# Linear attention woven into a feed-forward layer on one core: the second visit of attention split in two, and the copies of the solved values shared by two engines

## The chip, the cores and the metric

The program runs on one NeuronCore of a Trainium2 chip. Five engines work side by side, each through its own list of instructions in order: TensorE (PE in the tables; its weight loads stand apart as PEld), VectorE (DVE), ScalarE (ACT), GpSimd (POOL) and SyncE (SP, which here issues nearly all transfers). They meet only at semaphores. The metric is the device time of one execution in microseconds (us). Lower is better.

## The reference

Two parts, one behind the other. Attention is a delta rule with a state of 48x48 per head, for 4 batches, 8 heads and 768 positions:

```
k_n = k / (np.linalg.norm(k, axis=-1, keepdims=True) + 1e-06)
for t in range(S):
    y[:, :, t] = np.einsum('bhd,bhde->bhe', q[:, :, t], state)
    v_old = np.einsum('bhde,bhd->bhe', state, kt)
    state = state + bt[:, :, :, None] * np.einsum('bhd,bhe->bhde', kt, vt - v_old)
```

Its output, laid out as 3072 tokens of 384 numbers, goes through a feed-forward layer with 2048 inner columns:

```
h = np.maximum(x @ w_in, 0.0)
return (h * h @ w_out).astype(np.float32)
```

All is float32.

## The kernel before

The 768 positions are cut into 12 **units** of 64 (`u` = 0 to 11). Within a unit the recurrence is solved as a triangular system of 64 rows for each of the 32 pairs of batch and head. VectorE inverts the two 32-row halves of the triangle step by step (`invert`, L542 and L543), a unit ahead. TensorE puts the halves together and applies the result. The layer of unit `u - 1` runs on TensorE at the same time as the attention of unit `u`: the layer is long and made of large matmuls (128x128 weights, 256 or 384 columns), the attention is made of many small ones (32x32 to 64x64).

**The layer** (`moe`) of one unit has 8 rounds. A round makes one tile `h` with 18 matmuls (L756; in the changed file L762). ScalarE then takes Relu, Square and a rounded copy of it (`r`, `r`, `h_h`, L763 to L766), and VectorE the remainder (`h_l`, L735). Two rounds later 12 matmuls (L743; L749) add it to the outputs `o0` and `o1`.

**The attention** of a unit visits TensorE at fixed places between those rounds:

- first half of the corner: `h <- tt, ap` (L600; after the change L611), copied to `m` by ScalarE (L602);
- keys on the state: `x <- state, kq` (L639; L645), subtracted from the values `vt` by VectorE (L647);
- second half of the corner: `h <- m, t1` (L613; L623), written into `tt` by four ScalarE instructions (L617);
- queries on the state: `g <- state, kq` (L639; L645);
- the values solved: `x <- vt, tt` (L663; L669), copied back into `vt` (L665; L671);
- scores on them: `g <- vt, ap` (L677; L683), then keys on them, `x <- vt, kpad` (L695; L701), for the state.

The preparation of the unit two ahead (`prepared`, called `ahead`) takes a step behind some of these: transposes of its keys and queries (L353), two tiles into `x` and two into `h`, copied to `kq` by ScalarE (L356), then products of them (L369) and masked copies by VectorE (`ap`, L379). Units 10 and 11 have no unit to prepare.

**What sets the order.** The scheduler is off; every engine gets its instructions in the order in which the code issues them. `weave` merges generators by a table of places between 0 and 1. The layer has 32 places in a unit, and `CHAIN`, in 32nds, says where the attention comes in:

```
def two_visits(d, ahead):
    ahead = ahead or iter(())
    corner_rows(d)
    yield
    for _ in whole(d):
        pass
    take(ahead, 1)
...
CHAIN = (15.5, 17.5, 25.5)
```

So at 15.5 VectorE transposes the corner (`t1`, L563), at 17.5 the whole of `whole` is issued (the **second visit**), and at 25.5 everything from the solved values on (the **third visit**). The tile `h` has two buffers in PSUM, shared by the layer, both halves of the corner and the transposes; `x` has two of its own. Each of these buffers is handed on in turn.

Of the kernel before, what the change touches and what calls it, by code (L numbers as in the profile page):

```python
# [8 lines left out]
F32 = mybir.dt.float32  # L9
# [12 lines left out]
def kernel(  # L22
# [22 lines left out]
    nc = tc.nc  # L45
    B, H, S, D = q.shape
    DM, DF = w_in.shape
    P = 128
    C = 64
    HB = 32  # L50
# [11 lines left out]
    apool = ctx.enter_context(tc.tile_pool(name="attn", bufs=2))  # L62
# [34 lines left out]
    ttile = []  # L97
    for i in range(2):
        tt = const.tile([P, NC, H, C], F32, name=f"tt{i}")
# [212 lines left out]
    def x_tile(u=2):  # L312

        turn[0] += 1
        pool, name = (ps_h, "h") if u <= 1 and split_early and turn[0] % 4 >= 2 else (ps_x, "x")
        return pool.tile([P, PC], F32, name=name)
# [243 lines left out]
    def corner_rows(d):  # L560

        d["t1"] = apool.tile([P, H, HB], F32, name="t1", bufs=1)
        nc.vector.transpose(out=d["t1"], in_=d["t1t"])  # L563
        return d["t1"]

    def whole(d):

        u, ap = d["u"], d["ap"]
        tt = ttile[u % 2]
        upper = [slice(b * C, b * C + HB) for b in range(2)]  # L570
        lower = [slice(b * C + HB, (b + 1) * C) for b in range(2)]

        if not u:

            low, t1 = d["low"], d["t1"]
            m = mpool.tile([P, H2, HB], F32, name="x_l", bufs=1)
            ps = ps_h.tile([P, PC], F32, name="h").rearrange("p (h t) -> p h t", h=H2)
            for h in range(H2):
                for b in range(2):
                    nc.tensor.matmul(ps[upper[b], h], lhsT=ap[lower[b], h // H, h % H, 0, :HB], rhs=low[lower[b], h],  # L580
                                     start=True, stop=True)
            for b in range(2):
                nc.scalar.copy(out=m[upper[b]], in_=ps[upper[b]])
            yield
            ps = x_tile(u).rearrange("p (h t) -> p h t", h=H2)
            for h in range(H2):
                for b in range(2):
                    nc.tensor.matmul(ps[upper[b], h], lhsT=t1[upper[b], h], rhs=m[upper[b], h], start=True, stop=True)
            for b in range(2):
                nc.scalar.mul(out=tt.rearrange("p c h t -> p (c h) t")[upper[b], :, HB:], in_=ps[upper[b]], mul=-1.0)  # L590
            yield
            return
        t1 = d["t1"] if "t1" in d else corner_rows(d)
        m = apool.tile([P, H, HB], F32, name="m", bufs=1)
        at = [upper, lower]
        ps = ps_h.tile([P, PC], F32, name="h")[:, :H * HB].rearrange("p (k t) -> p k t", k=H)
        for h in range(H2):
            c, e = h // H, h % H
            for b in range(2):
                nc.tensor.matmul(ps[at[h % 2][b], h // 2], lhsT=ap[lower[b], c, e, 0, :HB],  # L600
                                 rhs=tt[lower[b], c, e, HB:], start=True, stop=True)
        nc.scalar.copy(out=m, in_=ps)  # L602
        if u == 1:
            yield
        keys_on_state(d)
        if u < MERGED - 2:
            yield
        ps = [(x_tile(u) if u < MERGED - 2 else ps_h.tile([P, PC], F32, name="h"))[:, :H * HB]
              .rearrange("p (k t) -> p k t", k=H) for _ in range(2)]
        for h in range(H2):  # L610
            for b in range(2):  # L611
                rows = at[h % 2][b]
                nc.tensor.matmul(ps[h % 2][upper[b], h // 2], lhsT=t1[rows, h // 2], rhs=m[rows, h // 2], start=True, stop=True)  # L613
        right = tt.rearrange("p c (k j) t -> p j (c k) t", j=2)
        for j in range(2):
            for b in range(2):
                nc.scalar.mul(out=right[upper[b], j, :, HB:], in_=ps[j][upper[b]], mul=-1.0)  # L617
        if u == 1:
            yield
        queries_on_state(d)  # L620
        yield

    def areas(two, n):  # L623

        return [x[:, :NC * n * D].rearrange("p (c n e) -> p c n e", c=NC, n=n) for x in two]

    def by_parity(x):

        return [x.rearrange("p c (n j) e -> p j c n e", j=2)[:, j] for j in range(2)]
# [12 lines left out]
    def keys_on_state(d):  # L642

        ks = areas([x_tile() for _ in range(2)], NP)
        on_state(d, 0, ks)  # L645
        for left, old in zip(by_parity(d["vt"]), ks):
            nc.vector.tensor_tensor(out=left, in0=left, in1=old, op=ALU.subtract)  # L647

    def queries_on_state(d):

        d["g"] = g = ps_g.tile([P, 2, PC], F32, name="g")
        on_state(d, 1, areas([g[:, j] for j in range(2)], NP))

    def solved(d):

        u, vt, tt = d["u"], d["vt"], ttile[d["u"] % 2]
        tv = areas([x_tile(u) for _ in range(2)], NP)
        for c in range(NC):
            for h in range(H):
                p, j = h // 2, h % 2  # L660
                for b in range(2):
                    rows, to = slice(b * C, (b + 1) * C), slice((b ^ j) * C, ((b ^ j) + 1) * C)
                    nc.tensor.matmul(tv[j][to, c, p], lhsT=tt[rows, c, h], rhs=vt[rows, c, h], start=True, stop=True)  # L663
        for new, old in zip(by_parity(vt), tv):
            nc.scalar.copy(out=new, in_=old)  # L665

    def scores_on_solved(d):

# [117 lines left out]
    def take(gen, n=None):  # L786
        while n is None or n > 0:
            try:
                next(gen)
            except StopIteration:  # L790
                return
            if n is not None:
                n -= 1
# [40 lines left out]
    def state_part(d):  # L834
        yield from whole(d)
        solved(d)
        yield
        onward(d)
        yield

    def two_visits(d, ahead):

        ahead = ahead or iter(())
        corner_rows(d)
        yield
        for _ in whole(d):
            pass
        take(ahead, 1)
        yield
        solved(d)  # L850
        take(ahead, 1)
        scores_on_solved(d)
        take(ahead, 1)
        if d["u"] < units - 1:
            keys_on_solved(d)
        yield
# [1 line left out]
    STEPS = 32  # L858
    OVER = 4
    MERGED = 4  # L860
    CHAIN = (15.5, 17.5, 25.5)
    CHAIN1 = (14.4, 17, 19.5, 21.5, 23.5, 27)
    L1, N1, N2 = 0.01, (0.36, 0.76), (0.03, 0.42)
    NI, SPANS = HB, {1: (0.54, 1.14), 2: (0.5, 1.12)}
# [1 line left out]
    ds_ = []  # L866
# [4 lines left out]
    with tc.manual_schedule(engines=engines):  # L871
# [47 lines left out]
        chain = state_part(ds_[0])  # L919
# [27 lines left out]
        for u in range(1, units):  # L947
            parts = []
            begun, ended = SPANS.get(u, (0.42, 1.1))
            n_i = round((1 - begun) / (ended - begun) * NI)  # L950
            if inverse:
                parts.append((inverse, left))
            getting, now = loads(u), moe(ds_[u - 1]) if u > 1 else first
            parts += [(now, [-2])] if u > 1 else []
            if u < MERGED - 1:
                parts.append((static(ds_[u + 1]), [-1, 0.155, 0.165, 0.17] if u > 1 else [0.12, 0.2, 0.21, 0.215]))
            elif ahead:
                parts.append((ahead, [-1, 0.13, 0.17]))
            ahead = prepared(u + 2) if 1 < u < units - 2 else None
            inverse = invert(ds_[u + 1]) if u < units - 1 else None  # L960
            if inverse:
                parts.append((inverse, steps(n_i, begun, 1)))
                left = steps(NI - n_i, 0, ended - 1) + [0.16 if u == 1 else 0.15]
            if u == 1:
                parts.append((corner, [0.04, 0.09, 0.1]))
                parts.append((third, [0.01, 0.015, 0.03, 0.045]))
                parts.append((late_loads(), [0.08]))
                parts.append((splits, steps(3 * (NW - FIRST) + 3 - used, 0, 0.72)))
                parts.append((pair[1], [0.25]))
            parts.append((getting, [L1] + steps(6, *N2) + [0.72, 0.93] if u + 2 < units else []) if u > 1 else  # L970
                         (getting, [0.09] + steps(6, *N1) + [0.93, 0.94]))
            chain = two_visits(ds_[u], ahead) if u > 1 else state_part(ds_[u])
            parts.append((chain, [x / STEPS for x in (CHAIN if u > 1 else CHAIN1)]))
            if before:
                parts += [(before, [x / STEPS for x in range(OVER)] + [0.2, 0.21])]
            parts.append((now, [x / STEPS for x in range(OVER, STEPS)] if u > 1 else steps(STEPS - OVER, 0, 1)))
            weave(*parts)
            before = now
# [34 lines left out]
```

## Time and profile before

| | before |
|---|---|
| median of three timed runs | 659.32 us (657.95 to 663.64) |
| the profiled execution | 661.13 us, of it span 659.4 us |
| TensorE busy | 601.3 us, 91% of the span |
| VectorE busy | 426.2 us, 65% |
| ScalarE busy | 317.2 us, 48% |
| mean granted TensorE clock | 0.951 of full speed |

The span is the time between the first and the last instruction of the profiled execution. An engine's busy time is the sum of its instructions. The granted clock is what the throttle let TensorE have: 1.00 is 2.4 GHz and 0.50 is 1.2 GHz. One profiled execution is one sample; the median of three others stands beside it.

### The profile page before, as it was taken

What the parts mean: (1) busy time and instruction counts of PE and PEld (TensorE: products, weight loads), DVE (VectorE), ACT (ScalarE), POOL (GpSimd) and SP (SyncE); (2) the same over time, 40 slices, a digit from 0 to 9 for tenths busy, and PEclk for the clock granted to TensorE, in tenths of its full rate; (3) what the DMA queues carried; (4) which work ended last, traced back from release to release, by engine and by line L of the source; (5) the groups of instructions that cost most, each with busy time, mean ns of one, the idle gap of its engine ahead of it and who ended that gap; (6) DMA issues with size and microseconds to landing.
All of it is one profiled execution on the core that took longest, in us unless ns stands there. A gap on an engine that the chain in (4) does not pass through costs nothing.

```text
span 659.4 us, 23855 instructions
## 1 busy us (share of the span) xinstructions
PE 601.3 (91%) x10392; PEld 570.6 (87%) x10392; DVE 426.2 (65%) x1131; ACT 317.2 (48%) x621; POOL 30.8 (5%) x52
## 2 busy tenths in 40 slices
PE   2948898998998999999999999999999999998997
PEld 2537787998998998998998998998998998898996
DVE  4795878886487676576587676775875855831121
ACT  4746675555345354354354354445444343354442
POOL 4000100001001000010001010010010010000000
PEclk9957697998999997998999999999999997999999
DMA  7797544035235244143134253143161051030100
GB/s 233 180 273 159 179 85 86 16 63 109 41 52 103 45 79 78 29 88 73 29 75 82 45 88 70 36 84 73 35 107 33 3 110 29 2 65 3 25 1 24
DMA packets 172464, 49.31 MB, mean 75 GB/s; under 512 B 164288, under 2 KB 167368, under 8 KB 172360
## 3 DMA queue, kind: packets, MB, share of 16 engines
q1 hardware_dynamic: 168840, 47.06, 34.1%
q8 instruction: 81, 1.33, 0.8%
q10 hardware_dynamic: 3392, 0.72, 0.6%
q14 instruction: 23, 0.19, 0.1%
q0 software_dynamic: 128, 0.01, 0.0%
HBM read 36.54 MB, written 10.49 MB: 71 GB/s over the span
## 4 chain that ended last, share of the span: by engine, by line
PE 80%; ACT 10%; issue 4%; DMA 3%; DVE 2%; SPq 1%; ACTq 0%; DVEq 0%
PE o L743 32%; PE h L756 31%; PE g L639 2%; PE x L369 2%; ACT r L764 2%; PE g L677 2%; ACT r L763 2%; ACT h_h L766 2%; PE x L353 1%; PE h L613 1%; PE x L695 1%; DMA kpad<-in_k_dram 1%; ACT vt L665 1%; PE h L722 1%; PE h L353 1%
## 5 line engine op out<-in xcount | busy, mean ns | idle before, releaser
L743 PE MATMUL o<-w,h_h 128*128 128x384 f32 x768 | 205.9, 350 | 0.0
L756 PE MATMUL h<-x_h,w 128*128 128x256 f32 x1152 | 170.7, 284 | 0.0
L763 ACT ACTIVATE r<-h 128x512 f32<-128x512 f32 x96 | 57.4, 598 | 231.6 <-PE h L756 231.2
L735 DVE TENSOR_TENSOR h_l<-r,h_h 128x512 fp32r<-128x512 f32 x96 | 68.3, 711 | 150.9 <-ACT h_h L766 150.3
L756 PEld LDWEIGHTS h<-x_h,w 128*128 128x128 f32 x1152 | 157.1, 192 | 0.6
L743 PEld LDWEIGHTS o<-w,h_h 128*128 128x128 f32 x768 | 139.0, 193 | 2.4
L743 PE MATMUL o<-w,h_l 128*128 128x384 f32 x384 | 132.4, 345 | 0.0
L542 DVE SCALAR_TENSOR_TENSOR tmp<-lt,bt,z 128x126 f32<-128x126 f32 (+22 forms) x310 | 96.8, 312 | 10.9 <-DMA lt<-blocks 2.6
L756 PE MATMUL h<-x_l,w 128*128 128x256 f32 x576 | 100.3, 283 | 0.0
L543 DVE TENSOR_TENSOR z<-z,tmp 128x126 f32<-128x126 f32 (+22 forms) x310 | 79.2, 255 | 10.7
L756 PEld LDWEIGHTS h<-x_l,w 128*128 128x128 f32 x576 | 82.8, 191 | 0.0
L743 PEld LDWEIGHTS o<-w,h_l 128*128 128x128 f32 x384 | 74.1, 193 | 0.0
L764 ACT ACTIVATE r<-r 128x512 f32<-128x512 f32 x96 | 60.7, 632 | 3.1
L766 ACT CAST h_h<-r 128x512 fp32r<-128x512 f32 x96 | 59.6, 620 | 3.0
L531 POOL MEMSET z<- 128x512 f32 x10 | 5.3, 527 | 470.9 <-DMA inv<-z 272.4
L677 PE MATMUL g<-vt,ap 64*64 64x48 f32 x768 | 17.7, 221 | 7.7 <-ACT vt L665 5.4
L677 PEld LDWEIGHTS g<-vt,ap 64*64 64x64 f32 x768 | 14.6, 134 | 10.7 <-ACT vt L665 8.6
L700 DVE TENSOR_TENSOR state<-state,x 48x384 f32<-48x384 f32 x40 | 22.0, 550 | 2.6 <-PE x L695 2.0
L356 ACT COPY kq<-x 128x512 f32<-128x512 f32 x25 | 13.6, 592 | 16.1 <-PE x L353 16.1
L369 PE MATMUL x<-kq 48*64 48x64 f32 (+1 forms) x608 | 19.5, 256 | 1.2 <-ACT kq L356 0.7
L617 ACT ACTIVATE tt<-h 32x256 f32<-32x256 f32 x40 | 14.9, 373 | 11.6 <-PE h L613 11.2
L639 PE MATMUL g<-state,kq 48*64 48x48 f32 x704 | 16.0, 237 | 4.5 <-issue 4.5
(147 smaller groups left out, 644.9 us busy)
## 6 DMA issues: line engine op xcount, KB each, us to landing
w<-in_moe_w_in_dram SPq DMA_DIRECT2D x12, 512.0 KB
w<-in_moe_w_out_dram SPq DMA_DIRECT2D x16, 384.0 KB
lt<-blocks SPq DMA_DIRECT2D x20, 256.0 KB
qpad<-in_q_dram SPq DMA_DIRECT2D x96, 48.0 KB
vt<-in_v_dram SPq DMA_DIRECT2D x48, 96.0 KB
out_dram<-a SPq DMA_DIRECT2D x46, 96.0 KB
kpad<-in_k_dram SPq DMA_DIRECT2D x88, 48.0 KB
blocks<-ap SPq DMA_DIRECT2D x40, 64.0 KB
```

The lines of the kernel that those rows point to most:

```text
L369: nc.tensor.matmul(ps[j][to * C:(to + 1) * C, p, (x - first) * C:(x - first + m) * C], lhsT=kq[rows, c, p, b, 0], rhs=kq[rows, c, p, b, x: ...
L542: nc.vector.scalar_tensor_tensor(out=tmp, scalar=bt[:, s:s + 1], op0=ALU.mult, op1=ALU.mult, **factors)
L543: nc.vector.tensor_tensor(out=z[:, :nj, s + 1:], in0=z[:, :nj, s + 1:], in1=tmp, op=ALU.subtract)
L639: nc.tensor.matmul(dst[j][to, c, p], lhsT=d["kq"][rows, c, p, b, x], rhs=state[rows, b, c, p], start=(c == 0 and p == 0) if x else True, s ...
L677: nc.tensor.matmul(gy[j][to, c, p], lhsT=ap[rows, c, h, 1], rhs=uu[rows, c, h], start=(u == 0 and c == 0 and p == 0), stop=True, skip_grou ...
L700: nc.vector.tensor_tensor(out=state[rows, b], in0=state[rows, b], in1=ku[b][rows], op=ALU.add)
L735: nc.vector.tensor_tensor(out=h_l, in0=r, in1=h_h.bitcast(F32), op=ALU.subtract)
L743: nc.tensor.matmul(o[i], lhsT=a[:, e, i * P:(i + 1) * P], rhs=halves["wo", ft][w], start=(ft == 0 and n == 0), stop=(ft == FT - 1 and n == 2))
L756: nc.tensor.matmul(hp[:, e], lhsT=halves["wi", (kt, ft // EACH)][w][:, f], rhs=x[:, kt], start=(n == 0), stop=(n == 3 * KT - 1))
L763: nc.scalar.activation(out=r, in_=hp, func=AF.Relu)
L764: nc.scalar.activation(out=r, in_=r, func=AF.Square)
L766: nc.scalar.copy(out=h_h, in_=r)
```

## The change

The second visit is cut. Its first half (first half of the corner, keys on the state) is issued at 15.5, one `h` group of the layer earlier than before. The transposed corner `t1` is made at 16.5. The second half of the corner, the queries and the step of `ahead` follow at 19.5, behind one `h` group and 12 `o` matmuls of the layer. The third visit stays at 25.5; for units 10 and 11, which prepare nothing, the scores and what follows are issued at 27.5. Of the two copies of the solved values, the one for odd heads goes to VectorE (units 2 to 11). Unit 0 and unit 1 keep their order.

```
-        t1 = d["t1"] if "t1" in d else corner_rows(d)
-        m = apool.tile([P, H, HB], F32, name="m", bufs=1)
...
+        corner_rows(d)
+        first_of_corner(d)
+        yield
+        keys_on_state(d)
+        yield
+        second_of_corner(d)
+        yield
+        queries_on_state(d)
+        yield
+
+    def first_of_corner(d):
+
+        ap, tt = d["ap"], ttile[d["u"] % 2]
+        d["m"] = m = apool.tile([P, H, HB], F32, name="m", bufs=1)
         ps = ps_h.tile([P, PC], F32, name="h")[:, :H * HB].rearrange("p (k t) -> p k t", k=H)
         for h in range(H2):
             c, e = h // H, h % H
             for b in range(2):
...
+                nc.tensor.matmul(ps[at[h % 2][b], h // 2], lhsT=ap[at[1][b], c, e, 0, :HB],
+                                 rhs=tt[at[1][b], c, e, HB:], start=True, stop=True)
         nc.scalar.copy(out=m, in_=ps)
...
+    def second_of_corner(d):
+
+        u, t1, m, tt = d["u"], d["t1"], d["m"], ttile[d["u"] % 2]
         ps = [(x_tile(u) if u < MERGED - 2 else ps_h.tile([P, PC], F32, name="h"))[:, :H * HB]
               .rearrange("p (k t) -> p k t", k=H) for _ in range(2)]
...
         for new, old in zip(by_parity(vt), tv):
-            nc.scalar.copy(out=new, in_=old)
+            (nc.vector.tensor_copy if u > 1 and old is tv[1] else nc.scalar.copy)(out=new, in_=old)
...
-    def two_visits(d, ahead):
-
-        ahead = ahead or iter(())
+    def three_visits(d, ahead):
+
+        more, ahead = ahead is not None, ahead or iter(())
+        first_of_corner(d)
+        keys_on_state(d)
+        yield
         corner_rows(d)
         yield
-        for _ in whole(d):
-            pass
+        second_of_corner(d)
+        queries_on_state(d)
         take(ahead, 1)
         yield
         solved(d)
-        take(ahead, 1)
+        if more:
+            take(ahead, 1)
+        else:
+            yield
         scores_on_solved(d)
         take(ahead, 1)
         if d["u"] < units - 1:
...
-    CHAIN = (15.5, 17.5, 25.5)
+    CHAIN = (15.5, 16.5, 19.5, 25.5, 27.5)
```

On TensorE in unit 6, around the second visit, before (`x32` counts rows that read alike; each of these small matmuls stands as two in the trace):

```order
L756 MATMUL h<-x_l,w_1203 128x256
L600 MATMUL h<-tt_108,ap 32x32 x32
L639 MATMUL x<-state,kq 64x48 x32
L613 MATMUL h<-m,t_5841 32x32 x32
L639 MATMUL g<-state,kq 64x48 x32
L353 MATMUL x<-plus,kpad_104 128x64 x8
L353 MATMUL x<-plus,qpad 128x64 x8
L353 MATMUL h<-plus,kpad_104 128x64 x8
L353 MATMUL h<-plus,qpad 128x64 x8
L743 MATMUL o_5655<-w_733,h_h 128x384 x2
```

and after; the two gaps are the rest of an `h` group of 18 and of the 12 `o` matmuls:

```order
L611 MATMUL h<-tt_108,ap 32x32 x32
L645 MATMUL x<-state,kq 64x48 x32
L762 MATMUL h<-x_h,w_1039 128x256
...
L749 MATMUL o_5655<-w_733,h_h 128x384 x2
...
L623 MATMUL h<-m,t_5924 32x32 x32
L645 MATMUL g<-state,kq 64x48 x32
L353 MATMUL x<-plus,kpad_104 128x64 x8
L353 MATMUL x<-plus,qpad 128x64 x8
L353 MATMUL h<-plus,kpad_104 128x64 x8
L353 MATMUL h<-plus,qpad 128x64 x8
L762 MATMUL h<-x_h,w_1039 128x256
```

One `h` group and the `o` matmuls that stood on either side of the visit now stand inside it, and the transposes, which were followed by `o` matmuls, are followed by an `h` group.

On VectorE in the third visit of unit 5, before (the steps of `invert`, then the masked copies for `ahead`):

```order
L542 SCALAR_TENSOR_TENSOR tmp<-lt,bt,z 128x126
L543 TENSOR_TENSOR z<-z,tmp 128x9x14
L379 TENSOR_TENSOR ap<-h,mask 128x4x128 x2
L700 TENSOR_TENSOR state<-state,x 48x384 x4
L735 TENSOR_TENSOR h_l<-r,h_h 128x512
```

and after:

```order
L542 SCALAR_TENSOR_TENSOR tmp<-lt,bt,z 128x126
L543 TENSOR_TENSOR z<-z,tmp 128x9x14
L671 COPY vt<-x 128x8x48
L379 TENSOR_TENSOR ap<-h,mask 128x4x128 x2
L706 TENSOR_TENSOR state<-state,x 48x384 x4
```

The copy of the odd heads stands behind the steps of `invert` that were already ahead of the masked copies.

On TensorE in the third visit of unit 10, before:

```order
L663 MATMUL x<-vt,tt_108 64x48 x32
L677 MATMUL g<-vt,ap 64x48 x32
L695 MATMUL x<-vt,kpad_102 48x48 x32
L743 MATMUL o_8920<-w_1312,h_h 128x384 x2
L743 MATMUL o_8920<-w_1312,h_l 128x384
```

and after, with the rest of the 12 `o` matmuls in the gap:

```order
L669 MATMUL x<-vt,tt_108 64x48 x32
L749 MATMUL o_8920<-w_1312,h_h 128x384 x2
...
L749 MATMUL o_8921<-w_1411,h_l 128x384
L683 MATMUL g<-vt,ap 64x48 x32
L701 MATMUL x<-vt,kpad_102 48x48 x32
```

Twelve `o` matmuls now lie between the solved values and the scores that read their copies; unit 11 is alike, without keys.

SP's and GpSimd's lists are the same in both kernels.

## Rows read from the trace of the kernel before

**Rows 1.** The page, parts 1 and 3: engines, and TensorE's instruction queue.
```profile
PE 601.3 (91%) x10392; PEld 570.6 (87%) x10392; DVE 426.2 (65%) x1131; ACT 317.2 (48%) x621; POOL 30.8 (5%) x52
...
q8 instruction: 81, 1.33, 0.8%
```

**Rows 2.** TensorE's waits: line <- releaser: us in total, times, longest.
```profile
PE g L677 <- ACT vt L665: 5.4, 10, 1.3
PE h L613 <- issue: 5.1, 5, 1.5
PE h L613 <- ACT m L602: 4.8, 10, 0.5
PE g L639 <- issue: 4.5, 5, 1.1
```

**Rows 3.** Timeline, second visit of unit 6: start us, us, instruction, [idle before <- releaser].
```profile
353.32 0.75 PE L600 MATMUL h<-tt,ap 32*32 32x32 f32 x64
...
355.67 0.72 PE L613 MATMUL h<-m,t 32*32 32x32 f32 x60 [0.51 <-ACT m L602]
...
357.20 0.25 PE L613 MATMUL h<-m,t 32*32 32x32 f32 x4 [0.81 <-issue]
...
358.46 0.46 PE L353 MATMUL x<-plus,kpad 64*128 64x64 f32 x8
...
359.20 1.07 ACT L356 COPY kq<-x 128x512 f32<-128x512 f32 x2 [0.96 <-PE x L353]
...
359.61 0.62 PE L743 MATMUL o<-w,h_h 128*128 128x384 f32 x2
...
360.16 1.10 ACT L356 COPY kq<-h 128x512 f32<-128x512 f32 x2
```

**Rows 4.** The chain that ended last, after the visits of units 5 and 6.
```profile
310.64 4.14 PE o L743 x12
...
359.68 2.31 PE o L743 x12
361.99 2.14 PE h L756 x18
```

**Rows 5.** Second visits by windows: last three columns are granted clock, DMA share, GB/s.
```profile
160.00:166.00 6.00, 5.65 (x109) 5.40 (x109) 3.97 (x15) 2.80 (x6) 0.00 (x0) 0.72 0.34 80
...
307.00:316.00 9.00, 8.01 (x79) 7.67 (x71) 3.14 (x11) 2.81 (x7) 0.00 (x0) 0.62 0.40 84
...
353.00:362.00 9.00, 7.67 (x306) 7.10 (x305) 6.74 (x22) 5.67 (x12) 0.00 (x0) 1.00 0.30 65
```

**Rows 6.** Timeline of TensorE: where the second visits of units 5 and 7 begin.
```profile
303.14 0.75 PE L600 MATMUL h<-tt,ap 32*32 32x32 f32 x64
...
400.88 0.78 PE L600 MATMUL h<-tt,ap 32*32 32x32 f32 x64
```

**Rows 7.** Timeline, third visits of units 5 and 10.
```profile
323.68 1.51 PE L677 MATMUL g<-vt,ap 64*64 64x48 f32 x64 [0.35 <-ACT vt L665]
324.06 1.01 PEld L677 LDWEIGHTS g<-vt,ap 64*64 64x64 f32 x60 [0.19 <-ACT vt L665]
...
325.24 1.29 DVE L379 TENSOR_TENSOR ap<-h,mask 128x512 f32<-128x512 f32 x2 [1.31 <-PE g L677]
...
562.75 1.46 PE L677 MATMUL g<-vt,ap 64*64 64x48 f32 x62 [1.30 <-ACT vt L665]
```

**Rows 8.** All waits: VectorE at the masked copies.
```profile
DVE ap L379 <- PE g L677: 12.3, 8, 2.1
```

**Rows 9.** One line's instructions: duration ns min/median/max.
```profile
L778 DVE COPY a<-o x12: 547/551/558, 145.8 to 654.6; 128x384 f32<-128x384 f32 x12
```

**Rows 10.** SP's waits, the row for the inverse's way back from DRAM.
```profile
SPq L553 <- DMA inv<-z: 13.1, 11, 2.3
```

**Rows 11.** Timeline of SP and TensorE before the second visit of unit 3.
```profile
199.94 1.97 SPq L558 DMA_DIRECT2D t1t<-inv  x4
...
205.06 0.75 PE L600 MATMUL h<-tt,ap 32*32 32x32 f32 x64
```

More of the change, by code (lines that the diff above doesn't have):

```diff
@@ L563, in corner_rows @@
         nc.vector.transpose(out=d["t1"], in_=d["t1t"])
-        return d["t1"]
+    at = [[slice(b * C + x * HB, b * C + (x + 1) * HB) for b in range(2)] for x in range(2)]
     def whole(d):
@@ L569, in whole @@
         tt = ttile[u % 2]
-        upper = [slice(b * C, b * C + HB) for b in range(2)]
-        lower = [slice(b * C + HB, (b + 1) * C) for b in range(2)]
+        upper, lower = at
         if not u:
@@ L592, in whole @@
             return
-        t1 = d["t1"] if "t1" in d else corner_rows(d)
-        m = apool.tile([P, H, HB], F32, name="m", bufs=1)
-        at = [upper, lower]
+        corner_rows(d)
[10 more added lines that the diff above has]
+        d["m"] = m = apool.tile([P, H, HB], F32, name="m", bufs=1)
         ps = ps_h.tile([P, PC], F32, name="h")[:, :H * HB].rearrange("p (k t) -> p k t", k=H)
@@ L599, in whole @@
             for b in range(2):
-                nc.tensor.matmul(ps[at[h % 2][b], h // 2], lhsT=ap[lower[b], c, e, 0, :HB],
-                                 rhs=tt[lower[b], c, e, HB:], start=True, stop=True)
+                nc.tensor.matmul(ps[at[h % 2][b], h // 2], lhsT=ap[at[1][b], c, e, 0, :HB],
+                                 rhs=tt[at[1][b], c, e, HB:], start=True, stop=True)
         nc.scalar.copy(out=m, in_=ps)
[L603 to L607, printed above, removed]
+    def second_of_corner(d):
+        u, t1, m, tt = d["u"], d["t1"], d["m"], ttile[d["u"] % 2]
         ps = [(x_tile(u) if u < MERGED - 2 else ps_h.tile([P, PC], F32, name="h"))[:, :H * HB]
@@ L612, in whole @@
                 rows = at[h % 2][b]
-                nc.tensor.matmul(ps[h % 2][upper[b], h // 2], lhsT=t1[rows, h // 2], rhs=m[rows, h // 2], start=True, stop=True)
+                nc.tensor.matmul(ps[h % 2][at[0][b], h // 2], lhsT=t1[rows, h // 2], rhs=m[rows, h // 2], start=True, stop=True)
         right = tt.rearrange("p c (k j) t -> p j (c k) t", j=2)
@@ L616, in whole @@
             for b in range(2):
[L617 to L621, printed above, removed]
+                nc.scalar.mul(out=right[at[0][b], j, :, HB:], in_=ps[j][at[0][b]], mul=-1.0)
     def areas(two, n):
@@ L971 @@
                          (getting, [0.09] + steps(6, *N1) + [0.93, 0.94]))
-            chain = two_visits(ds_[u], ahead) if u > 1 else state_part(ds_[u])
+            chain = three_visits(ds_[u], ahead) if u > 1 else state_part(ds_[u])
             parts.append((chain, [x / STEPS for x in (CHAIN if u > 1 else CHAIN1)]))
```

## The prediction

> **What bounds the kernel now.** I read the page first. TensorE is busy 601.3 of 659.4 us, VectorE 426.2 [rows 1]: TensorE sets the time, so the change is worth what it removes of TensorE's idle time and of its time at half clock. Next the waits of TensorE [rows 2]. In the ten units 2 to 11 the second visit waits once for `m` (4.8 us in 10 waits) and stands still once for "issue", that is for nothing the profile shows (5.1 and 4.5 us, five each). The third visit waits for the copies of the solved values (5.4 us, of which units 10 and 11 have 1.3 each). Then the timeline of one second visit, unit 6 [rows 3]: it begins at 353.32, waits 0.51 us for `m`, stands 0.81 us in the middle of the second corner half, ends at 359.61 with the first `o` matmul of the layer. Last the granted clock. It is 1.00 through the visit of unit 6, but 0.72 and 0.62 in the stretches of units 2 and 5, and 0.62 again in two like stretches, 256 to 265 and 546 to 555, of units 4 and 10 [rows 5]. There TensorE falls to 1.2 GHz within the visit, after small matmuls broken by the two stalls, and the 12 `o` matmuls behind it take 4.14 us instead of 2.31 [rows 4]. No other visit of units 2 to 11 shows a fall.
>
> **The parts, one by one.** All against the profiled execution's own 661.1 us.
>
> *The wait for `m`.* The second corner half now stands 18 `h` and 12 `o` matmuls behind the first, 2.14 and 2.31 us [rows 4]. The copy of `m` needs only some 0.5 us. All goes: **-4.8 us** [rows 2].
>
> *The issue stalls.* TensorE's instruction queue fetched 81 packets for 10,392 matmuls and as many weight loads [rows 1]: 20,784 / 81 = 257 instructions a packet. In unit 6 the stall comes after 376 instructions of the visit (64 + 64 matmuls, then 60 of the next 64, each with its load) [rows 3]. In the odd units it comes in the queries, 128 later. So I read the stall as the wait for the next packet. The packet before began 119 instructions into the visit, near 354.0, and the stall ended at 357.2: a packet takes some 3.2 us to come, and 257 small instructions last less. The change puts 60 instructions that last 4.4 us into the middle. In even units a packet then spans keys, `h`, `o` and corner, some 5.6 us, no stall. In odd units it spans most of the first half and the `h` group: 0.55 of the corner's 0.7 us, 1.1 of keys (353.32 to 355.67, less 0.51 and 0.7) [rows 3] and 2.1, together 3.7 us, just enough. I take **-9.2** of the 9.6; the bounds are -7 and -9.6.
>
> Here the Trainium skill speaks against me: Runtime: NRT & Kernel Launch, "Instruction fetch mechanics", gives blocks of 256 instructions, which fits the 257, but says that fetching is hidden behind the pace of issue. By that the stalls would have another cause and could stay, and the sum would lose the 9.2 us. The stalls at a fixed count [rows 3] speak for the fetch.
>
> *A new wait.* Before, the transposes for `ahead` were followed by 12 `o` matmuls. Now an `h` group follows at once, and its tile is one that the transposes have just filled: it is free when ScalarE has made the first `kq <- h` copy. In unit 6 the transposes end at 359.61; ScalarE starts the two `kq <- x` at 359.20 and the two `kq <- h` at 360.16, which take 1.10 together, so the first is done near 360.76 [rows 3]. TensorE will wait 1.15 us, in the eight units 2 to 9 that transpose: **+9.2 us**, bounds 0.8 and 1.4 each, so 6.4 and 11.2. ScalarE can't be earlier: the copies wait for the transposes, and the four `tt` writes end about then. Behind the waiting `h` group stands the whole layer. Units 10 and 11 have no transposes and no such wait.
>
> *Third visits of units 10 and 11.* The scores waited 1.30 us each for the copies [rows 7]; 12 `o` matmuls, 2.1 us, now lie between. **-2.6 us**.
>
> *The copy on VectorE.* In unit 5 the scores started 0.35 us late, with the first copy, and the second cost another 0.19 [rows 7]. The first copy doesn't move, since ScalarE is busy with the layer until then. VectorE went idle 1.31 us before it could mask at 325.24, at 323.93, that is 0.25 us behind the start of the scores; its in-order list puts the new copy there. A VectorE copy of 128x384 out of PSUM takes 0.551 us [rows 9], so the odd heads are there 0.85 us after the start instead of 0.38: 0.47 us more wait. The eight such idles sum to 12.3 us, longest 2.1 [rows 8]; only unit 2, with the 2.1, is early enough to gain, some 0.2. 7 x 0.47 - 0.2 = **+3.1 us**, bounds 0 and 5.6. TensorE waits there with the scores, the keys and the layer queued behind; the masked copies wait for the scores as before.
>
> *The earlier first half.* It needs `tt` 2.1 us sooner. In unit 3 its four transfers are issued by 199.94 and the visit began at 205.06 [rows 11], so the new place is 202.9. The like transfer `inv <- z` kept SP waiting up to 2.3 us behind its successor's issue [rows 10]. If `tt` lands 2.4 to 3.8 us after its issue it is sometimes just late: **+0.5 us**, bounds 0 and 3. The subtraction and `t1` on VectorE keep 2 us or more until they are read; cost nothing.
>
> *The clock.* The visits of units 5, 6 and 7 begin at 303.14, 353.32 and 400.88 [rows 3, 6]: 50.2 us with a fall, 47.6 without, **2.6 us a fall**. Three falls at 0.62 and a shorter one at 0.72 make 3.5 of them, 9.1 us; the windows' upper bound, (1 - clock) x length, is 11.9. After the change no stretch of small matmuls is longer than some 4 us, with one wait of 1.15 us at its end, where the visits of [rows 3] had 6.3 us with two stalls. I expect the falls to go but for 0.3 of one: **-8.3 us**.
>
> Sum: -4.8 - 9.2 + 9.2 - 2.6 + 3.1 + 0.5 - 8.3 = **-12.1 us**, 649.0 us. The median of the timed runs is 1.8 us lower than the profiled execution, less than one fall; with 0.7 falls fewer before, the gain there is some 10.3, which again gives 649.0. Without the clock the edits nearly cancel: what two stalls give back, the wait behind the transposes takes.
>
> **The rivals.**
>
> *The falls stay.* Unit 6 had both stalls and kept its clock, unit 5 had both and lost it [rows 4, 5], so length of a visit doesn't decide alone. If the half with transposes and the wait behind them still falls about as often, 8.3 us are lost: 649.0 + 8.3 = 657.3 us. The Trainium skill, TensorE: Matmul & The Clock Gate, "A second HAM failure mode", says that short idles between matmul groups, where PSUM banks are cycled, make the clock swing; the wait that the change adds is such an idle. Unit 6 shows that such idles need not do it. For the rival: four falls in ten with stalls of this size. Against: the third visit, which has a wait of its own in all ten units [rows 2], shows no fall in any. Chance 0.17.
>
> *The clock falls in every second half* (the side of slower). Place: the transposes and the 1.15 us of standing behind them, in units 2 to 9. Price 2.6 us each, 8 x 2.6 = 20.8 in place of the 0.8 that I kept: 649.0 + 20.0 = 669.0 us. It decides above some five falls (12.1 / 2.6 beyond those I kept). Chance 0.07.
>
> *The stalls are not the fetch.* They stay at their places in the list and the 9.2 us don't come: 658.2 us. Chance 0.09.
>
> **How the numbers follow.** The forecast has 0.67. Within it the bounds give 642 (wait of 0.8, VectorE's copy free, no fall) to about 657 (1.4, 5.6, 3 and issue -7). The two rivals of no gain lie at 657 and 658, so 642 to 658 leaves out little more than the slower one. 1%, about what a measurement of this kernel can tell from no change, is 6.6 us, so faster means under 652.7. The forecast lies 3.7 under it and falls there some 9 times in 10: 0.61. The rest of it, and the two rivals, 0.32, is within 1%. Slower: 0.07.
>
> **What would show it.** The waits for `m` gone; issue rows at the corner and the queries gone or under 0.3 us; a new wait of an `h` group on `kq` of some 1.15 us, eight times; the scores' wait on VectorE's copy near 0.8 us behind their start; the scores of units 10 and 11 without wait; granted clock 1.00 behind the second visits of all ten units. Wrong if the issue stalls reappear elsewhere, if `tt` is late in most units, or if the clock column still shows 0.6.

## The result and the profile after

| | before | after |
|---|---|---|
| median of the timed runs | 661.28 us (657.95 to 663.64, 4 runs) | 643.78 us (642.22 to 645.89, 4 runs) |
| the profiled execution | 661.13 us, span 659.4 us | 644.14 us, span 642.4 us |
| mean granted clock | 0.951 | 0.966 |

The ratio is 0.974, with an interval of 0.968 to 0.980: faster. The kernel before has one timed run more here than in the table ahead of the prediction. Medians here and below hold every run; the ratios leave out runs more than 1.5% above the fastest of the same kernel. The span became 17.0 us shorter, where the sum of the forecast had 12.1.

The page of the changed kernel, parts 1 to 3:

```profile
span 642.4 us, 23854 instructions
PE 589.4 (92%) x10392; PEld 557.1 (87%) x10392; DVE 431.9 (67%) x1141; ACT 314.7 (49%) x611; POOL 31.3 (5%) x52
...
PEclk9966698999999999999999999999999999999999
...
q8 instruction: 81, 1.33, 0.8%
```

TensorE executes as many instructions and fetches as many packets as before [rows 1], but is busy 11.9 us less; the terms further down put some 10 us of it down to the higher clock. From the eighth slice on the clock column shows only 9s; in windows of 1 us the granted clock is 1.00 in each from 125 to 640 us. TensorE's waits (line <- releaser: us in total, times, longest), to be held against [rows 2]:

```profile
PE h L762 <- ACT kq L356: 8.0, 8, 1.1
...
PE g L683 <- DVE vt L671: 3.1, 7, 0.5
PE g L683 <- ACT vt L671: 2.8, 8, 0.4
...
PE x L701 <- issue: 0.5, 1, 0.5
```

The wait for `m` and the issue rows of the second corner half and of the queries are gone. The first row shown is new: the wait behind the transposes, eight times 1.0 us. The last is one stall in a third visit, that of unit 2; the kernel before has three of 0.2 us in third visits. The timeline of unit 6, TensorE and ScalarE, answers to [rows 3]:

```profile
343.98 0.75 PE L611 MATMUL h<-tt,ap 32*32 32x32 f32 x64
344.66 1.15 PE L645 MATMUL x<-state,kq 48*64 48x48 f32 x64
344.78 0.37 ACT L613 COPY m<-h 128x256 f32<-128x256 f32 x1 [0.89 <-PE h L611]
...
350.19 0.75 PE L623 MATMUL h<-m,t 32*32 32x32 f32 x64
350.88 1.15 PE L645 MATMUL g<-state,kq 48*64 48x48 f32 x64
350.96 1.55 ACT L627 ACTIVATE tt<-h 32x256 f32<-32x256 f32 x4 [0.86 <-PE h L623]
352.70 1.07 ACT L356 COPY kq<-x 128x512 f32<-128x512 f32 x2 [0.19 <-PE x L353]
353.66 1.09 ACT L356 COPY kq<-h 128x512 f32<-128x512 f32 x2
354.31 0.98 PE L762 MATMUL h<-x_h,w 128*128 128x256 f32 x6 [1.05 <-ACT kq L356]
```

Each half runs through without a stop. The copy of `m` is done at 345.15, five microseconds before it is read. ScalarE is never idle for long between 350.96 and 354.75 (the `tt` writes, then four copies), and the `h` group starts when the first of the two `kq <- h` is done. The granted clock (last column but two), in stretches with the second visits of units 2, 5, 6 and 10, answers to [rows 5]:

```profile
148.00:163.00 15.00, 15.00 (x339) 14.30 (x339) 9.36 (x25) 7.57 (x15) 2.28 (x3) 1.00 0.61 105
297.00:306.00 9.00, 9.00 (x310) 8.45 (x295) 7.47 (x25) 4.28 (x10) 0.00 (x0) 1.00 0.33 72
344.00:358.00 14.00, 12.95 (x346) 12.37 (x346) 8.53 (x27) 6.99 (x14) 0.00 (x0) 1.00 0.37 76
533.00:542.00 9.00, 9.00 (x295) 8.38 (x294) 7.40 (x24) 3.79 (x9) 0.00 (x0) 1.00 0.43 92
```

It is 1.00 in all four, as in the other six visits. Last the third visits of units 6 and 11 in the timeline, which answer to [rows 7]:

```profile
363.35 0.32 PE L683 MATMUL g<-vt,ap 64*64 64x48 f32 x4 [0.35 <-ACT vt L671]
363.51 0.55 DVE L671 COPY vt<-x 128x384 f32<-128x384 f32 x1
364.12 1.08 PE L683 MATMUL g<-vt,ap 64*64 64x48 f32 x58 [0.45 <-DVE vt L671]
...
593.00 1.15 PE L683 MATMUL g<-vt,ap 64*64 64x48 f32 x64
```

In unit 6 TensorE stops twice, for each copy once; in unit 11 not at all.

### The profile page after: what moved, and what is told of

Its sections match the earlier page's. It is cut to its first block, busy times and chain, and to the rows that moved or that the text cites. A ratio compares the mean times of both kernels' runs of the same rounds, so it can differ in the third digit from the quotient of the medians.

```text
span 642.4 us, 23854 instructions
## 1 busy us (share of the span) xinstructions
PE 589.4 (92%) x10392; PEld 557.1 (87%) x10392; DVE 431.9 (67%) x1141; ACT 314.7 (49%) x611; POOL 31.3 (5%) x52
## 4 chain that ended last, share of the span: by engine, by line
PE 76%; DVE 8%; ACT 7%; DMA 5%; issue 2%; SPq 2%; ACTq 0%; DVEq 0%
PE h L762 30%; PE o L749 29%; DVE tmp L542 2%; ACT kq L356 2%; PE g L683 2%; DVE z L543 2%; PE x L645 2%; PE x L369 2%; DMA w<-in_moe_w_out_dram 2%; PE g L645 2%; PE x L353 1%; PE x L701 1%; PE h L623 1%; PE h L611 1%; DMA w<-in_moe_w_in_dram 1%
## 5 line engine op out<-in xcount | busy, mean ns | idle before, releaser
L749 PE MATMUL o<-w,h_h 128*128 128x384 f32 x768 | 200.6, 342 | 0.0
L762 PE MATMUL h<-x_h,w 128*128 128x256 f32 x1152 | 172.8, 286 | 8.0 <-ACT kq L356 8.0
L762 PEld LDWEIGHTS h<-x_h,w 128*128 128x128 f32 x1152 | 155.0, 191 | 10.5 <-ACT kq L356 9.1
L749 PEld LDWEIGHTS o<-w,h_h 128*128 128x128 f32 x768 | 135.7, 189 | 1.6
L749 PE MATMUL o<-w,h_l 128*128 128x384 f32 x384 | 130.3, 339 | 0.0
L749 PEld LDWEIGHTS o<-w,h_l 128*128 128x128 f32 x384 | 72.4, 189 | 0.0
L683 PE MATMUL g<-vt,ap 64*64 64x48 f32 x768 | 16.1, 221 | 6.9 <-DVE vt L671 3.1
L687 ACT COPY y<-g 128x384 f32<-128x384 f32 x24 | 10.3, 482 | 23.1 <-PE g L683 23.1
L369 PEld LDWEIGHTS x<-kq 48*64 48x64 f32 x608 | 16.6, 147 | 2.8 <-ACT kq L356 1.1
```

The costliest lines, as they stand in the source:

```text
L369: nc.tensor.matmul(ps[j][to * C:(to + 1) * C, p, (x - first) * C:(x - first + m) * C], lhsT=kq[rows, c, p, b, 0], rhs=kq[rows, c, p, b, x: ...
L683: nc.tensor.matmul(gy[j][to, c, p], lhsT=ap[rows, c, h, 1], rhs=uu[rows, c, h], start=(u == 0 and c == 0 and p == 0), stop=True, skip_grou ...
L749: nc.tensor.matmul(o[i], lhsT=a[:, e, i * P:(i + 1) * P], rhs=halves["wo", ft][w], start=(ft == 0 and n == 0), stop=(ft == FT - 1 and n == 2))
L762: nc.tensor.matmul(hp[:, e], lhsT=halves["wi", (kt, ft // EACH)][w][:, f], rhs=x[:, kt], start=(n == 0), stop=(n == 3 * KT - 1))
```

## The experiments

The theory: the split ends the issue stalls, since fewer instructions lie in the time that a packet needs; it ends the wait for `m`; and with both gone the clock keeps its level. The copies and the late scores are small. The rivals are those of the prediction. Times are medians with lowest and highest; a ratio is to the kernel before, timed on the same chip. The variants ran on three chips, where the kernel before had medians of 661.74, 666.03 and 662.36 us; a variant and the changed kernel were not timed side by side, so a difference between their times is less sure than a ratio. Every trace is of one execution. A fall is a stretch in which the granted clock goes from 1.00 to 0.50.

### The split alone

The changed kernel without its two edits to the third visit:

```
-            (nc.vector.tensor_copy if u > 1 and old is tv[1] else nc.scalar.copy)(out=new, in_=old)
+            nc.scalar.copy(out=new, in_=old)
...
-        if more:
-            take(ahead, 1)
-        else:
-            yield
+        take(ahead, 1)
...
-    CHAIN = (15.5, 16.5, 19.5, 25.5, 27.5)
+    CHAIN = (15.5, 16.5, 19.5, 25.5)
```

> Only the second visit is split; both copies of the solved values stay with ScalarE and the scores of units 10 and 11 follow at once. My theory, the parts add up and the split carries the change: no wait for m, no issue stall in the second visit, eight waits of an h group for kq of about 1.0 us, granted clock 1.00 in all ten units, so 661.3 - 4.8 - 9.6 + 8.0 - 9.8 = about 645 us, 0.975 of before. Rival, the clock falls come and go by chance and have nothing to do with the split: the stalls alone give 661.3 - 6.4 = about 655 us, 0.990, and the clock column shows 0.6 behind some second visits.

645.62 us (644.89 to 646.52), ratio 0.979 (0.975 to 0.983). The wait on `kq` is 8.1 us in 8, the scores wait 5.4 us in 10 for ScalarE as before, and no unit from 2 on has a fall. The split makes nearly the whole gain: some 16 of 17.5 us.

### The copy on VectorE alone, in the kernel before

```
-            nc.scalar.copy(out=new, in_=old)
+            (nc.vector.tensor_copy if u > 1 and old is tv[1] else nc.scalar.copy)(out=new, in_=old)
```

> The kernel before with nothing but the copy of the odd heads moved to VectorE. My theory: VectorE reaches it a quarter of a microsecond behind the start of the scores, which costs 0.26 us in each of units 3 to 9 and gains 0.2 in units 2, 10 and 11: plus 1 to 2 us, 1.002 of before, and the falls of the clock stay. Rival, two engines share a load that was on the path: minus 2 to 3 us, 0.996.

670.17 us (663.41 to 673.63), ratio 1.0125 (1.0035 to 1.0216): slower, and more so than expected, though by how much is not settled. The waits of this kernel show the price in the last row (before, ScalarE's second copy had cost 0.19 us each time [rows 7], 1.5 us in eight), and stalls that are 2.4 us longer together than before:

```profile
PE h L613 <- issue: 7.0, 5, 2.0
PE g L677 <- ACT vt L665: 5.4, 10, 1.3
PE g L639 <- issue: 5.0, 5, 1.5
PE h L613 <- ACT m L602: 4.8, 10, 0.5
PE g L677 <- DVE vt L665: 3.6, 8, 0.5
```

The rest goes with the clock: the profiled execution (673.63 us, the slowest of its runs) has nine falls and a mean of 0.932. The 3.6 us are the copy's, some 2 more than ScalarE's had cost; whether the additional falls are due to it or to chance, this run can't tell. One of the nine stands outside the second visits, behind the wait of the scores in unit 10's third visit.

### The late scores alone, in the kernel before

The scores of units 10 and 11 at 27.5 (`CHAIN = (15.5, 17.5, 25.5, 27.5)`, and the `if more` of the change).

> The kernel before with nothing but the scores of units 10 and 11 issued 12 o matmuls later. My theory: two waits of 1.30 us and two of 0.19 us go, minus 2.6 to 3.0 us, 0.996 of before; the falls of the clock in the other units stay. Rival, ScalarE or the bank of the layer makes it wait elsewhere: no change.

661.66 us (658.65 to 665.12), ratio 1.0004 (0.997 to 1.0038). The waits of 1.3 us are gone (the scores wait 2.8 us in 8 now), but the gain isn't in the time. The interval just leaves out the whole 2.6 us (0.996), so something took it back, and the granted clocks point to the falls: 0.945 on average over these ten runs, 0.949 over the thirteen of the kernel before, with six falls in the profiled execution. Whether the edit brings more falls or chance did, this run can't tell; in the unsplit kernel the falls hide a gain of this size.

### Sixty-four instructions more at the start

The kernel before, with the 32 transposes that unit 0's preparation makes at L353 made twice (work without use, far ahead of the units in question):

```
-                for p in range(NP):
+                for p in [p for _ in range(2 if u == 0 else 1) for p in range(NP)]:
```

> The kernel before with the 32 transposes of unit 0 made twice, so 64 more instructions on TensorE near the start and nothing else. My theory, the issue stalls are the wait for the next packet of 257 instructions: all stalls move 64 instructions ahead in the visits of units 2 to 11, from behind the 60th matmul of the second corner half (even units) and of the queries (odd units) to behind about the 28th, and last about as long. Rival, the stall belongs to the work at that place: it stays behind the 60th.

669.3 us, one run, not compared in time. What matters is where the stalls are. Two second visits in its timeline, of units 3 and 4:

```profile
212.56 0.89 PE L639 MATMUL g<-state,kq 48*64 48x48 f32 x36 [1.16 <-issue]
...
258.98 0.44 PE L613 MATMUL h<-m,t 32*32 32x32 f32 x28 [0.51 <-ACT m L602]
260.29 0.50 PE L613 MATMUL h<-m,t 32*32 32x32 f32 x36 [0.88 <-issue]
```

In the kernel before the stall of unit 4 stands behind 60 of the 64 matmuls:

```profile
255.18 0.72 PE L613 MATMUL h<-m,t 32*32 32x32 f32 x60 [0.51 <-ACT m L602]
256.93 0.32 PE L613 MATMUL h<-m,t 32*32 32x32 f32 x4 [1.03 <-issue]
```

32 matmuls more with their 32 loads, and the stall comes 32 matmuls with their loads earlier in each unit: behind 28 instead of 60, in unit 2 behind 30 instead of 62, in unit 11 behind 29 instead of 61. Its place hangs on the count of instructions from the start of the program and on nothing that happens in the visit. The kernel before shows the count too: between the starts of one stall and the next lie from 508 to 1784 matmuls and loads, and in all twelve gaps from unit 2 on that is a whole number times 254 to 256. Those are the packets of some 257; the rival by which the stalls have another cause than the fetch falls. Whether a packet is late, and by how much, does depend on what stands ahead of it: in the second visits after the change it isn't.

### Queries ahead of the corner, without a split

The kernel before, the visit in one piece, with the queries issued ahead of the second corner half in units 2 to 11, so that they cover the copy of `m`:

```
         if u < MERGED - 2:
             yield
+        else:
+            queries_on_state(d)
...
         if u == 1:
             yield
-        queries_on_state(d)
+            queries_on_state(d)
```

> The kernel before, its second visit in one piece, but the queries on the state are issued ahead of the second half of the corner: 64 matmuls more stand between the first half and the read of m. Theory (the stalls hang on the count of instructions, the falls on the long visit with its stalls): the wait for m goes, -4.8 us; the issue stalls stay at the same count, now in the corner in the odd units and in the queries in the even ones; falls stay, 4 to 9. Time 656 (652 to 662). Rival (the wait for m is what starts the falls): the falls go too, and the time is 645 to 648.

672.58 us (666.63 to 673.41), ratio 1.014 (1.005 to 1.023). The waits:

```profile
PE g L641 <- issue: 7.5, 5, 2.0
...
PE h L615 <- issue: 6.5, 5, 1.5
```

The wait for `m` is gone, and the stalls changed places between queries and corner, as expected. But they are longer: 14.0 us together, where stalls and wait together had been 14.4 [rows 2]. I read that as a packet that comes when it comes: what TensorE did not spend on `m`, it spent on the packet. It is one execution; in the four traces with the wait for `m` the stalls sum to 8.9 to 12.0 us. And the clock fell in eight units from 2 on, four times as in [rows 5] and four times for less (windows as in [rows 5]):

```profile
356.00:366.00 10.00, 9.14 (x127) 8.64 (x127) 3.30 (x11) 3.64 (x8) 0.00 (x0) 0.66 0.35 75
405.00:415.00 10.00, 8.61 (x196) 8.24 (x189) 5.10 (x15) 4.00 (x10) 0.00 (x0) 0.83 0.34 72
```

Both my size (656) and the rival's (645 to 648) were wrong: taking this wait out of the unsplit visit gained nothing, the runs are even slower, at clocks of 0.930 to 0.943, and the falls don't need the wait for `m`.

### The wait behind the transposes, doubled

The changed kernel, the two `kq <- x` copies made twice by ScalarE in the preparation of later units:

```
-            for b in range(2):
+            for b in (0, 1, 0, 1) if u >= MERGED and parts[0][0] == 0 else (0, 1):
```

> The changed kernel, but ScalarE makes the two copies of the x tiles into kq twice in the preparation of later units (the second time is work without use), so that the copy for which the h group behind the transposes waits ends some 1.1 us later. This takes the disputed wait and doubles it. Theory (the wait costs its length and leaves the clock alone): 8 waits of some 2.1 to 3.2 us instead of 1.0 in the units where it stands, so +8 to +17 us, 652 to 661, granted clock 1.00 throughout. Rival of the forecast (standing behind the transposes is what makes the clock fall): falls of 2.7 us behind these waits, up to +20 us more, so 670 and over, with clocks of 0.6 in the windows behind the second halves.

658.92 us (656.27 to 663.57), ratio 0.994 (0.989 to 0.998): 15 us over the changed kernel. Its wait, the place in unit 6's timeline, and windows behind two of the second visits:

```profile
PE h L762 <- ACT kq L356: 15.8, 8, 2.0
```

```profile
361.77 0.97 PE L762 MATMUL h<-x_h,w 128*128 128x256 f32 x6 [2.04 <-ACT kq L356]
362.58 0.53 PE L762 MATMUL h<-x_l,w 128*128 128x256 f32 x3
362.93 1.46 PE L762 MATMUL h<-x_h,w 128*128 128x256 f32 x6
...
367.63 0.87 PE L762 MATMUL h<-x_h,w 128*128 128x256 f32 x6
```

```profile
210.00:220.00 10.00, 7.96 (x143) 7.77 (x138) 4.11 (x13) 6.38 (x13) 0.00 (x0) 1.00 0.36 74
...
360.00:370.00 10.00, 8.23 (x58) 8.10 (x60) 3.34 (x10) 4.11 (x9) 0.00 (x0) 0.83 0.27 52
```

The wait costs its length, 7.8 us more. But behind five of the eight waits the clock now falls: six matmuls that take 0.87 us take 1.46. Of units 3 to 9 those with such a fall last 49.6 us on average and those without 48.3, so each costs 1.3. The time lies in the range of my theory (652 to 661), but by luck: that range had longer waits and no fall, and the runs have waits of 2.0 us and falls. The mechanism of the rival that ends slower is real, and was not reached: 1.0 us of standing gave no fall in eight units here, nor in the sixteen of the other two traces with this wait; 2.0 us gave one in five of eight. My theory that the wait leaves the clock alone holds for the wait that the change makes, no further.

### Twelve and six matmuls behind the transposes

The changed kernel with the second half at 17.5, and at 18.5:

```
-    CHAIN = (15.5, 16.5, 19.5, 25.5, 27.5)
+    CHAIN = (15.5, 16.5, 17.5, 25.5, 27.5)
```

> The changed kernel with the second half of the corner issued at 17.5, right behind the h group: all 12 matmuls for o stand behind the transposes, as before the change. Theory: the wait on kq goes wholly, -8.0 us; the cut in the middle is 2.1 us long instead of 4.3, so the packets in the odd units last some 1.8 us against 3.2 that a packet needs, and stalls of about 1.4 us come back in five units, +7. Without falls of the clock 643 (640 to 646). Rival (small matmuls with stalls among them make the clock fall, whatever the cut): some four falls, +11, so 654.

650.11 us (647.74 to 651.57), ratio 0.980 (0.972 to 0.987). The wait on `kq` is gone; these came for it:

```profile
PE h L623 <- ACT r L769: 4.8, 10, 0.5
...
PE g L645 <- issue: 3.3, 5, 1.0
...
PE h L353 <- ACT tt L627: 1.0, 4, 0.3
```

The stalls are back in the five odd units, for 3.3 us rather than 7. That may come of a wait that I had not seen, which now stands ahead of them: the second half follows the `h` group at once, and one of its two `h` tiles is that group's, free only after ScalarE's Relu. One fall, in unit 7; the timed runs have clocks of 0.960 to 0.969. It is 6 us slower than the change, not equal to it: the 643 expected had nothing of the new waits (4.8 and 1.0 us) and no fall.

> The changed kernel with the second half of the corner issued at 18.5 instead of 19.5, so that some 6 of the 12 matmuls for o stand behind the transposes of ahead instead of in front of the corner. Theory (the h group waits for the copy of the transposed tiles; 6 matmuls for o of 0.176 us are 1.06 us): the wait of 8.0 us on kq falls to under 1 us. The packets of the instruction queue that hold the middle of the visit then last some 1 us less, so stalls of up to 0.5 us come back in the five odd units, together at most 2.5 us. No fall of the clock in units 2 to 11. Time 638 (636 to 641), against 643.8 of the changed kernel. Rival (the split works only by its length): the falls come back in four units or more, 2.7 us each, and the time is 648 or more.

636.99 us (635.29 to 638.73), ratio 0.960 (0.953 to 0.967). In its timeline in unit 6 the next `h` group starts with no wait:

```profile
346.84 1.07 ACT L356 COPY kq<-x 128x512 f32<-128x512 f32 x2
347.42 0.62 PE L749 MATMUL o<-w,h_h 128*128 128x384 f32 x2
347.80 1.10 ACT L356 COPY kq<-h 128x512 f32<-128x512 f32 x2
...
348.58 0.88 PE L762 MATMUL h<-x_h,w 128*128 128x256 f32 x6
```

The wait of 8.0 us is gone, 1.2 us of stalls came back, no fall: 6.8 us less than the change. The price of the wait is shown by taking it away.

### Copies on ScalarE again, and all scores late

The changed kernel with VectorE's copy in units 10 and 11 alone (`u > 9` for `u > 1`):

> The changed kernel, but both copies of the solved values by ScalarE in units 2 to 9; VectorE copies the odd heads in units 10 and 11 alone, where 12 matmuls for o cover it. This prices the sharing of the copies in the changed kernel. My term was +3.1 us for it in these units; the traces since then say some 0.26 us for each of seven. Theory: the wait for VectorE's copy (3.1 us in 7) goes, that for ScalarE's grows from 2.8 to some 4.2, so -1.8 us, 642 against 643.8 of the changed kernel. Rival (sharing relieves ScalarE, which pays elsewhere): 643.8 or more.

642.21 us (640.29 to 643.22), ratio 0.968 (0.963 to 0.973). The 3.1 us of waits for VectorE are gone, and that for ScalarE stays at 2.8 (I had expected it to grow to 4.2). 1.6 us less than the change: near the 1.8 expected, but within the spread of the runs.

The same with the second half at 18.5:

> The last one with the second half of the corner at 18.5, six matmuls for o behind the transposes. Theory: both gains add, since they lie at different places: 637.0 of that place alone, less 1.8, so 635.2 (633 to 637). Rival (the issue stalls or falls come back, because units are then a little shorter): 638 or more.

636.44 us (635.27 to 639.76), ratio 0.961 (0.957 to 0.964); its stalls in the queries are 2.5 us. The second gain is not to be seen beside the first.

The same, and the scores at 27.5 in all units, as the change has it for units 10 and 11:

```
-        more, ahead = ahead is not None, ahead or iter(())
+        ahead = ahead or iter(())
...
-        if more:
-            take(ahead, 1)
-        else:
-            yield
+        take(ahead, 1)
+        yield
```

> The last one, with the scores and what follows at 27.5 in all units from 2 to 11, behind 12 matmuls for o, as the change did for units 10 and 11 alone. Theory: the scores' wait for the copies, some 5.4 us in eight units, goes too, and no fall of the clock appears: 630 to 632. Rival (the state, the masked copies and the next unit's first half come 2.1 us later and are now late, or the waits only move): 635 or more.

631.59 us (628.24 to 633.05), ratio 0.952 (0.949 to 0.956), 12 us under the change. Of the waits of units 2 to 11 this one is left:

```profile
PE g L645 <- issue: 1.7, 3, 1.0
```

The waits for the copies are gone, nothing later became late, and no unit from 2 on has a fall. It is the fastest of all the runs.

## Why the prediction was right

The forecast of 649.0 lies 5.2 us over the median, and the mechanism is the forecast one; the sizes that were off were all off to the same side, so none hid another. By its terms, in the profiled executions:

- *The wait for `m`*, -4.8: all gone.
- *The issue stalls*, -9.2: all 9.6 of the second visits gone. The shift by 64 instructions and the spacing of the stalls show that they are the fetch. So the passage cited from the Trainium skill (Runtime: NRT & Kernel Launch, "Instruction fetch mechanics") fits in its blocks of 256 (254 to 256 counted here) and not in its claim that fetching is hidden: here it costs up to 1.5 us at a time [rows 2].
- *The new wait*, +9.2: there, in the eight units named, 1.0 us each instead of 1.15, **+8.0**. Taking it away gave 6.8 back.
- *Third visits of units 10 and 11*, -2.6: the waits are gone, and it brought a little more. Unit 10 takes 44.5 us with the split alone and 43.0 after, unit 11 42.7 and 41.2, together **-3.1**. The run with ScalarE's copies in units 2 to 9 differs from the split alone in these two units only, and is 3.4 us faster, with spreads that don't meet (on two chips): in the split kernel such an amount is larger than the noise.
- *The copy on VectorE*, +3.1: mis-sized. The scores wait 0.45 us for it where ScalarE's second copy had cost 0.19 [rows 7], so eight units lose 3.1 - 8 x 0.19 = **+1.6 us**; undoing it gave 1.6 too, though the spread of the runs is as wide. From the start of the scores to the next `o` matmul these units sum to 20.6 us after, 19.3 and 19.6 in the two runs where ScalarE makes both copies, so it may be nearer 1.0 to 1.3.
- *The earlier first half*, +0.5: nothing; no unit waits for `tt`. The landing time of 2.4 to 3.8 us that the term supposed stands in no row.
- *The clock*, -8.3: mis-sized, **-10.0**. A unit is taken from its first transposes of `y` (L722; after the change L728) to those of the next: unit 5 from 282.21 to 332.39 before, 277.99 to 325.19 after. Units 3 and 6 to 9, without a fall on either side, became 0.3 us shorter on average; units 2, 4 and 5, which had falls, by 2.0, 3.0 and 3.0; unit 10, which had one, by 5.8 and unit 11, which had none, by 2.9. The differences give 1.7, 2.7, 2.7 and 2.9 us, together 10.0; and the 0.3 of a fall that I kept did not come.

With 3.1 for the third visits these terms make -17.9; the units up to 1 became 1.2 us longer, and some 0.3 of gain is not assigned. Without the clock I had the edits nearly cancel (-3.8); in fact they bring 7.9. The clock's term hangs on the execution that was profiled: it had four falls, the traces of the four other kernels with an uncut visit have six to nine. And the prediction's slow end was added up wrong: 1.4, 5.6, 3 and -7 give 658.2, not 657; nothing hangs on it.

Of the rivals, "the stalls are not the fetch" is refuted. "The falls stay" did not come true: the granted clocks of the runs are 0.965 to 0.973 after, and 0.934 to 0.956 in the 37 runs of the kernel before that were timed beside the experiments. "The clock falls in every second half" was nearer than its chance said: twice the wait makes it come in five units of eight. To that extent the other passage cited from the Trainium skill (TensorE: Matmul & The Clock Gate, "A second HAM failure mode", idles between matmul groups that make the clock swing) agrees with the doubled wait, and not with the change's own 1.0 us.

Against the falls the prediction had held that the third visit, with its own wait, shows none. That was so in the one trace it had. In the run with 64 instructions more, unit 11's third visit has one: two `o` matmuls that take 0.52 us at the full clock take 0.84 behind the 1.30 us that the scores wait.

```profile
614.16 1.51 PE L677 MATMUL g<-vt,ap 64*64 64x48 f32 x64 [1.30 <-ACT vt L665]
...
616.53 0.84 PE L743 MATMUL o<-w,h_h 128*128 128x384 f32 x2
```

Unit 10 has one in the run with the copy alone. The late scores take just these waits away; the run with the split alone keeps them and has no fall in its trace, so how often they would do it is open.

What decides in which unit the clock falls stays open. Unit 6 had both stalls and kept its clock; kernels with the visit in one piece fell in four to nine units, not the same ones each time. The runs show that the split ends the falls (with the cut at half its length one came back), and that a longer wait behind the small matmuls brings some back; they don't separate the length of the visit from the stalls in it, since no kernel here has a visit in one piece without stalls. The cut at half its length, with a wait of 0.5 us in all ten units, stalls of up to 1.0 us in five and one fall, speaks for the length, but is one trace.

## What to carry to other kernels

Stretches of many small matmuls are worth cutting with long ones: here that removed waits on copies, waits on instructions and time at half clock at once, while taking one wait out of the uncut stretch gave nothing: the stalls for the next packet of instructions were longer by nearly as much, and the falls stayed. When a cut puts a new group behind a copy, look for a place with a microsecond of other work in between: six `o` matmuls behind the transposes were worth 6.8 us, and twelve cost more than none. And the cover that the change gave to two units (scores behind 12 matmuls) was worth giving to all.

## What the runs showed of the hardware

- TensorE's instruction stalls keep their place to the instruction: 64 instructions more at the start moved those of all units by 64, and two stalls are a whole number of packets of 254 to 256 matmuls and loads apart. In one trace 14.4 us of stalls with a wait became 14.0 of stalls without it.
- The kernel before varies with its clock: those 37 runs go from 656.81 us at a mean clock of 0.956 to 670.01 us at 0.934. The kernels whose trace has no fall from unit 2 on are faster and seem steadier: 642.22 to 645.89 after, in four runs, and no more than 4.9 us from lowest to highest in the others.
- A fall behind a doubled wait (0.83 over 10 us) cost 1.3 us, one in the uncut visits 2.7: falls differ in size, so counting them is not enough.
